# Forming the expert table of the last layer in wider pieces, and moving squares from VectorE to ScalarE

## The chip, the cores and the metric

The kernel runs on one core of one Trainium2 chip. The metric is the time of one execution on the device, in microseconds. An execution of the profiled kind also leaves a trace: its span runs from the first to the last instruction, and its own time is a little longer.

## The reference, cut to what matters

Three layers follow each other: a linear attention with complex decay, a soft mixture of experts, and a dense layer with a squared relu. The change touches only the last two products of the mixture and the dense layer:

```
c = softmax over 32 slots of (x @ phi)            # 3072 tokens x 32
x = c @ slot_out                                  # slot_out: 32 x 384
h = max(x @ w_in, 0)                              # w_in: 384 x 2048
out = (h * h) @ w_out                             # w_out: 2048 x 384
```

All arrays are fp32; the two weights arrive as 64-bit floats and are decoded to fp32 on the chip.

## The kernel before

The first stages (attention, and the experts that give `slot_out`) fill the first 297 us and are not touched. Their instructions are issued in an order written out by hand. The last layer is issued in program order, so that each engine has one queue in the order of the code below.

The last layer doesn't form x. Since x @ w_in = c @ (slot_out @ w_in), it forms G = slot_out @ w_in, 32 slots by 2048, once. To keep fp32 accuracy with products in a shorter format (F32R), each factor is split in a rounded part and a rest. G is stored in 128 partitions: 32 slots four times, rounded in partitions 0 to 63 and the rest in 64 to 127. cT, the transposed softmax of 512 tokens, has rounded, rest, rounded, rest in its four groups of 32 partitions. One product of G and cT over 128 partitions then gives all four cross terms.

- `make_G(f)` forms one block of 128 columns of G: three fp32 products (two instructions each) with soT, the transposed `slot_out` repeated four times by `slots`; then a ScalarE copy that rounds, and a VectorE subtraction that puts the rest in the upper half.
- `spread_c(g)` (VectorE) and `make_cT(g)` (four TensorE transposes, one ScalarE copy, two VectorE subtractions of 32 partitions) prepare the tokens of group g, 512 of 3072.
- The work is cut into 96 steps n: a group g of six and a block f of 16. `seq` runs over f = 0 to 7 for all six groups first (the first pass, n = 0 to 47) and then over f = 8 to 15 (the second pass).
- `up_last(n)` multiplies block f of G with cT of group g, takes relu to s and square to sh (rounded), both on ScalarE, and the square once more in full fp32, q, on VectorE, or on ScalarE for n = 1 to 7. `split(n)` makes sl = q - sh on VectorE.
- Step n then adds nine products to the three banks `po`: sh with the rounded and the rest of w_out (L784), sl with the rounded (L781). `up_last` runs two steps and `split` one step ahead of that.
- `weights_out` and the generator `beside_last` decode the weights of both products beside this (for each block of 128: ScalarE `size`, four VectorE steps, and for w_out also a ScalarE copy `woh` and a VectorE subtraction `wol`). In steps 0 to 3 one block of w_out is decoded per step; from step 4 the rest is taken in pieces, 2.4 per step. In that stretch G's blocks 8 to 15 are made too.
- After the eighth step of a group `po` is copied out (first pass) or added and stored (second pass).

The order of a step, cut:

```
if n: split(n + 1)
if n < HALF: make_G(f + 5), weights_out(f + 4)      # each while its argument is under 8
pieces of beside_last
if f == 3: spread_c(g + 1)
if f == 5: make_cT(g + 1, wide)
up_last(n + 2)
nine products into po
```

PSUM holds four banks for `ph` (G, cT and the products of `up_last`) and four for `po`; s and q have three buffers, sh and sl four.

Of the kernel before, what the change touches and what calls it, by code (L numbers as in the profile page):

```python
# [12 lines left out]
F32 = mybir.dt.float32  # L13
# [3 lines left out]
AF = mybir.ActivationFunctionType  # L17
ALU = mybir.AluOpType
# [12 lines left out]
NS = NE * SPE  # L31
# [79 lines left out]
HALF, PACE = 8, 2.4  # L111
# [169 lines left out]
def moe_kernel(ctx, tc, raw, cst, aT, qk, vv_d, phi, w1, w2, w_in, w_out, out):  # L281
    nc = tc.nc
    mm = nc.tensor.matmul
    tr = nc.tensor.transpose
    V = nc.vector

    const = ctx.enter_context(tc.tile_pool(name="const", bufs=1))
# [2 lines left out]
    cn = const.tile([128, NU, NS], F32, name="cn")  # L290
    flags = const.tile([128, 3, NTU], F32, name="flags")
    acc = const.tile([128, DM], F32, name="acc")
    soT = const.tile([128, 3, 4, NS], F32, name="soT")
    mrun = const.tile([128, 1], F32, name="mrun")
    srun = const.tile([128, 1], F32, name="srun")
    siT = const.tile([128, 3, NS], F32, name="siT")
# [6 lines left out]
    def act(*args, **kw):  # L303
        return nc.scalar.activation(*args, **kw)  # L304
# [200 lines left out]
    def pools(ph):  # L505
        def pool(name, bufs, **kw):
            return ph.enter_context(tc.tile_pool(name=name, bufs=bufs, **kw))
        return pool
# [26 lines left out]
    def finish(weights, psum, ps_b, hid, p_raw, p_d, used, swap, check):  # L535
# [8 lines left out]
        def bank():  # L544
            return ps_b.tile([128, 512], F32, name="pt")
# [39 lines left out]
        def slots(g):  # L585
            p = bank()
            for kc in range(3):
                tr(p[:, 128 * kc:128 * (kc + 1)], so[g][:, 128 * kc:128 * (kc + 1)], ident)
            for r in range(4):
                V.tensor_copy(  # L590
                    soT[:, :, r, 16 * g:16 * g + 16].rearrange("p k (j s) -> p k j s", j=4),
                    p[:, :DM].rearrange("p (k j s) -> p k j s", k=3, j=4)[:, :, :, :SPE])
# [15 lines left out]
        jobs = [(1, f) for f in range(HALF)] + [(o, f) for f in range(HALF, 16) for o in (0, 1)]  # L608
# [8 lines left out]
        def decode(n):  # L617

            o, f = jobs[n]
            if o:  # L620
                R["dw", n] = dst = R["dw"].tile([128, 1, DM], F32, name="dw")
            else:
                dst = wi[:, :, 128 * f:128 * (f + 1)]
            sl = slice(f, f + 1)
            return [fn for _, fn in f64_steps(p_d, lambda: R["raw", n], dst)] + [
                lambda: load_job(n + 3)] + [
                lambda: act(R["woh"][:, sl], R["dw", n], AF.Copy),
                lambda: V.tensor_tensor(out=R["wol"][:, sl], in0=R["dw", n], in1=R["woh"][:, sl], op=ALU.subtract)] * o

        def pieces(steps):  # L630
            for fn in steps:
                fn()
                yield

        def weights_out(n):
            steps = decode(n)
            for fn in steps[:4] + R.pop("parts", []) + steps[4:6]:
                fn()
            R["parts"] = steps[6:]

        def spread_c(g):
            R["c4", g] = R["c4"].tile([128, 4, 4, NS], F32, name="c4")
            V.tensor_copy(R["c4", g], cn[:, 4 * g:4 * g + 4].unsqueeze(2).to_broadcast([128, 4, 4, NS]))
# [44 lines left out]
        with phC, ExitStack() as ph:  # L688
            pool = pools(ph)
            G = pool("p_G", 1).tile([128, DFF], F32R, name="G")  # L690
            p_r = pool("p_r", 3)
            p_h = pool("p_h", 4)
            p_o = pool("p_o", 1)
            R["c"] = pool("p_cs", 1)
            ps_h = pool("ps_h", 4, space=PSUM)
            ps_o = pool("ps_o", 4, space=PSUM)
            sp, sq = {}, {}

            def wide():
                return ps_h.tile([128, 512], F32, name="ph")  # L700

            def make_G(f):
                if f >= 16:
                    return
                p = wide()[:, :128]
                for kc in range(3):
                    mm(p, soT[:, kc].rearrange("p r s -> p (r s)"), wi[:, kc, 128 * f:128 * (f + 1)], start=kc == 0, stop=kc == 2)
                dst = G[:, 128 * f:128 * (f + 1)]
                act(dst, p, AF.Copy)
                V.tensor_tensor(out=dst[64:], in0=p[64:], in1=dst[64:], op=ALU.subtract)  # L710

            seq = [(g, f) for fs in (range(HALF), range(HALF, 16)) for g in range(6) for f in fs]

            def beside_last():

                yield from pieces(R.pop("parts"))
                for m in range(HALF, len(jobs), 2):
                    yield from pieces(decode(m))
                    steps = decode(m + 1)
                    yield from pieces(steps[:3])  # L720
                    make_G(jobs[m][1])
                    yield from pieces(steps[3:])
            rest, paced = beside_last(), [0]

            def up_last(n):
                if n >= len(seq):
                    return
                g, f = seq[n]
                p = wide()
                mm(p, G[:, 128 * f:128 * (f + 1)], R["cT", g], start=True, stop=True)  # L730
                s = p_r.tile([128, 512], F32, name="s")
                act(s, p, AF.Relu)
                sh = p_h.tile([128, 512], F32R, name="sh")
                act(sh, s, AF.Square)
                q = p_r.tile([128, 512], F32, name="q")
                if not 0 < n < 8:
                    V.tensor_tensor(out=q, in0=s, in1=s, op=ALU.mult)  # L737
                else:
                    act(q, s, AF.Square)
                sq[n] = q, sh  # L740

            def split(n):
                if n >= len(seq):
                    return
                s, sh = sq.pop(n)
                sl = p_h.tile([128, 512], F32R, name="sl")
                V.tensor_tensor(out=sl, in0=s, in1=sh, op=ALU.subtract)  # L747
                sp[n] = sh, sl

            make_G(0)  # L750
            make_G(1)
            up_last(0)
            make_G(2)
            split(0)
            up_last(1)
            make_G(3)
            split(1)
            make_G(4)
            po, o = None, {}
            for n, (g, f) in enumerate(seq):  # L760
                if f % HALF == 0:
                    po = [ps_o.tile([128, 512], F32, name="po") for _ in range(3)]
                if n:
                    split(n + 1)
                if n < HALF:
                    if f + 5 < HALF:
                        make_G(f + 5)
                    if f + 4 < HALF:
                        weights_out(f + 4)
                while paced[0] < (n - 3) * PACE and next(rest, True) is None:  # L770
                    paced[0] += 1
                if f == 3 and n < 5 * HALF:
                    spread_c(g + 1)
                if f == 5 and n < 5 * HALF:
                    make_cT(g + 1, wide)
                up_last(n + 2)
                sh, sl = sp.pop(n)
                fst, lst = f % HALF == 0, f % HALF == HALF - 1

                def low(c):  # L780
                    mm(po[c], R["woh"][:, f, 128 * c:128 * (c + 1)], sl, start=False, stop=lst)  # L781
                for c in range(3):
                    for w in ("woh", "wol"):
                        mm(po[c], R[w][:, f, 128 * c:128 * (c + 1)], sh, start=fst and w == "woh", stop=False)  # L784
                    if lst:
                        low(c)
                if not lst:
                    for c in range(3):
                        low(c)
                if n == 20:  # L790
                    check()
                if lst:
                    for c in range(3):
                        if f < HALF:
                            o[g, c] = p_o.tile([128, 512], F32, name=f"o{g}{c}")
                            copy("D" if c == 1 else "A", o[g, c], po[c])
                        else:
                            V.tensor_tensor(out=o[g, c], in0=po[c], in1=o[g, c], op=ALU.add)
                            nc.sync.dma_start(out=out[128 * c:128 * (c + 1), 512 * g:512 * (g + 1)], in_=o[g, c])

    wi = ctx.enter_context(tc.tile_pool(name="p_wi", bufs=1)).tile([128, 3, DFF], F32, name="wi")
# [5 lines left out]
    with tc.manual_schedule():  # L807
# [395 lines left out]
        n = N_PRE  # L1203
# [42 lines left out]
        def check():  # L1246
            in_range.append(nc.values_load(count[:1, :1], min_val=0, max_val=128))
# [59 lines left out]
```

## Time and profile before

| what | value |
|---|---|
| three runs | 549.75, 550.99, 555.09 us; median 550.99 |
| profiled execution | 551.92 us, of which the span is 550.1 |
| mean granted TensorE clock | 0.991 of full speed |
| TensorE, VectorE, ScalarE busy | 520.2, 447.4, 361.9 us |
| last layer | about 297 us to 543 us |

Busy times are sums of the durations of an engine's instructions where they don't overlap; those of TensorE overlap their successors, so that the distance between starts, not the duration, is the price of one.

### The profile page before, as it was taken

The numbers are of one execution on the slowest core, as the hardware profiler recorded it, in microseconds if no ns is written. First come the engines' busy times: TensorE is split into PE (matmuls) and PEld (weight loads), VectorE is DVE, ScalarE is ACT, GpSimd is POOL, SyncE is SP. The second block draws the span as 40 slices with busy tenths as digits, with TensorE's granted clock in tenths as the row PEclk, the third lists the DMA queues.
The fourth block names the chain that finished last, engine by engine and source line by source line (L and its number), as shares of the span: only waits on it lengthen the run. The fifth ranks groups of instructions, "written<-read, shape, count | busy, mean of one in ns | idle before, by whom it ended". The sixth has DMA issues, their size and how long they took to land.

```text
span 550.1 us, 10120 instructions
## 1 busy us (share of the span) xinstructions
PE 520.2 (95%) x4006; PEld 417.1 (76%) x4006; DVE 447.4 (81%) x774; ACT 361.9 (66%) x664; POOL 0.2 (0%) x4
## 2 busy tenths in 40 slices
PE   0999999999999999999799979999999999999994
PEld 0998888888788787888336768777788888888883
DVE  4899999999999987885567978998998975777672
ACT  6799999999889876522034766757676655555550
POOL 0000000000000000000000000000000000000000
PEclk9999999999999999999899989999999999999998
DMA  6432533470462226739993312110210010111011
GB/s 213 144 117 90 184 93 130 128 292 23 121 236 90 74 87 206 299 139 422 421 397 130 87 57 59 57 58 31 58 57 30 0 58 0 60 57 57 2 57 63
DMA packets 23958, 67.15 MB, mean 122 GB/s; under 512 B 2144, under 2 KB 12256, under 8 KB 21856
## 3 DMA queue, kind: packets, MB, share of 16 engines
q1 hardware_dynamic: 23904, 66.44, 34.4%
q8 instruction: 33, 0.54, 0.4%
q14 instruction: 21, 0.17, 0.1%
HBM read 61.71 MB, written 4.72 MB: 121 GB/s over the span
## 4 chain that ended last, share of the span: by engine, by line
PE 86%; DVE 9%; ACT 1%; DMA 1%; issue 1%; SPq 1%; DVEq 0%; ACTq 0%
PE po L784 21%; PE po L781 10%; PE pt L1047 9%; PE pt L1095 8%; PE py L1110 6%; PE pS L1072 5%; PE pt L1228 5%; PE ph L730 4%; PE pt L939 3%; PE py L1115 3%; PE pt L557 2%; PE pt L1131 2%; DVE sl L747 2%; PE pt L572 1%; PE pt L334 1%; DMA a<-in_a_dram 1%
## 5 line engine op out<-in xcount | busy, mean ns | idle before, releaser
L784 PE MATMUL po<-sh,wol 128*128 128x512 f32 x288 | 114.4, 397 | 0.0
L784 PE MATMUL po<-sh,woh 128*128 128x512 f32 x288 | 114.2, 397 | 0.0
L304 ACT ACTIVATE s<-ph 128x512 f32<-128x512 f32 x96 | 57.2, 596 | 63.1 <-PE ph L730 62.9
L737 DVE TENSOR_TENSOR q<-s 128x512 f32<-128x512 f32 x89 | 61.3, 689 | 32.5 <-ACT s L304 32.1
L781 PE MATMUL po<-sl,woh 128*128 128x512 f32 x288 | 86.5, 395 | 0.0
L747 DVE TENSOR_TENSOR sl<-q,sh 128x512 fp32r<-128x512 f32 x96 | 66.3, 691 | 10.9 <-ACT q L304 1.3
L781 PEld LDWEIGHTS po<-sl,woh 128*128 128x128 f32 x288 | 54.4, 189 | 13.2 <-DVE sl L747 0.2
L784 PEld LDWEIGHTS po<-sh,wol 128*128 128x128 f32 x288 | 54.6, 189 | 12.9
L784 PEld LDWEIGHTS po<-sh,woh 128*128 128x128 f32 x288 | 54.6, 190 | 12.2 <-ACT o L304 0.3
L304 ACT ACTIVATE sh<-s 128x512 fp32r<-128x512 f32 x96 | 60.8, 633 | 3.1
L304 ACT ACTIVATE T<-pt 96x512 f32<-96x512 f32 x83 | 47.4, 593 | 11.0 <-PE pt L1047 10.5
L1095 PE MATMUL pt<-T,T 96*128 96x128 f32 x384 | 52.7, 280 | 0.0
L1095 PEld LDWEIGHTS pt<-T,T 96*128 96x128 f32 x384 | 46.6, 192 | 3.3 <-issue 2.6
L730 PE MATMUL ph<-cT,G 128*128 128x512 f32 x96 | 40.0, 417 | 4.5 <-DVE cT L653 4.4
L1110 PE MATMUL py<-am,v 128*48 128x128 f32 x384 | 40.9, 291 | 0.0
L1099 DVE TENSOR_TENSOR am<-pt,cs 128x512 f32<-128x512 f32 x48 | 32.8, 685 | 6.7 <-PE pt L1095 6.1
L939 PE MATMUL pt<-cs,t 128*128 128x128 f32 x144 | 23.6, 282 | 12.7 <-DVE t L893 12.7
L1115 PE MATMUL py<-T,S 96*48 96x128 f32 x320 | 31.3, 273 | 0.0
L1072 PEld LDWEIGHTS pS<-v,KN 128*96 128x96 f32 x320 | 29.4, 165 | 2.0 <-issue 2.0
L314 ACT ACT_TABLE_LOAD x23 | 29.5, 1283 | 1.1 <-PEq L1298 0.7
L1072 PE MATMUL pS<-v,KN 128*96 128x48 f32 x320 | 30.0, 247 | 0.0
L1047 PE MATMUL pt<-cs,KN 128*96 128x128 f32 x192 | 29.9, 278 | 0.0
(153 smaller groups left out, 856.7 us busy)
## 6 DMA issues: line engine op xcount, KB each, us to landing
w<-in_w_dram SPq DMA_DIRECT2D x16, 1536.0 KB, 11.5
qk<-in_qk_dram SPq DMA_DIRECT2D x24, 384.0 KB, 3.1
a<-in_a_dram SPq DMA_DIRECT2D x14, 576.0 KB, 4.6
raw<-in_wi_dram SPq DMA_DIRECT2D x16, 384.0 KB, 3.2
raw<-in_wo_dram SPq DMA_DIRECT2D x16, 384.0 KB, 3.1
v<-in_vn_dram SPq DMA_DIRECT2D x24, 192.0 KB, 2.6
out_dram<-o SPq DMA_DIRECT2D x18, 256.0 KB, 2.2
a<-in_a_dram SPq DMA_DIRECT2D x2, 384.0 KB, 5.0
```

What stands on the lines that cost most here:

```text
L304: return nc.scalar.activation(*args, **kw)
L730: mm(p, G[:, 128 * f:128 * (f + 1)], R["cT", g], start=True, stop=True)
L737: V.tensor_tensor(out=q, in0=s, in1=s, op=ALU.mult)
L747: V.tensor_tensor(out=sl, in0=s, in1=sh, op=ALU.subtract)
L781: mm(po[c], R["woh"][:, f, 128 * c:128 * (c + 1)], sl, start=False, stop=lst)
L784: mm(po[c], R[w][:, f, 128 * c:128 * (c + 1)], sh, start=fst and w == "woh", stop=False)
L939: tr(pe[:, C * j:C * (j + 1)], x[:, j, C * i:C * (i + 1)], ident)
L1047: tr(pt[:96, C * h:C * (h + 1)], X[:, 4 * g + h].rearrange("p c d -> p (c d)"), ident)
L1072: mm(pS[:96, D * h:D * (h + 1)], st["KN", u][:, h].rearrange("p c d -> p (c d)"), st["v", u][:, h], start=not seeded, stop=not seeded or h ...
L1095: mm(p[:, C * h:C * (h + 1)], st["T", u, 1, g][:, h], st["T", u, 0, g][:, h], start=True, stop=True)
L1110: mm(p[64 * w:64 * w + D, C * pr:C * (pr + 1)], st["v", u][:, h], st["am", u, h // 4][:, h % 4], start=True, stop=fst)
L1115: mm(p[64 * w:64 * w + D, C * pr:C * (pr + 1)], st["S", u][:, h], st["T", u, 0, h // 4][:, h % 4], start=False, stop=True)
```

## The change

G is formed for four blocks at once. soT now holds the slots twice, so the weights have 64 columns. Two blocks go to partitions 0 to 63 of one PSUM bank and the next two to partitions 64 to 127, 256 columns each, the products of the two halves alternating. For each half a ScalarE copy then writes the rounded part to partitions 0 to 63 of G and a VectorE subtraction the rest to 64 to 127. G(0) and G(4) are formed before step 0, the other two groups when the last of their four blocks of w_in is being decoded.

The square q goes to VectorE where n is a multiple of 3 or at least 45, otherwise to ScalarE. `spread_c` is moved from the fourth step of a group to the third (f = 2), `make_cT` from the sixth to the fifth (f = 4).

```diff
-    soT = const.tile([128, 3, 4, NS], F32, name="soT")
+    soT = const.tile([128, 3, 2, NS], F32, name="soT")
...
-            for r in range(4):
+            for r in range(2):
...
-            def make_G(f):
-                if f >= 16:
-                    return
-                p = wide()[:, :128]
+            def make_G(f, n=2):
+                p = wide()[:, :128 * n]
+                halves = [(p[64 * j:64 * j + 64], slice(128 * (f + n * j), 128 * (f + n * j + n))) for j in range(2)]
                 for kc in range(3):
-                    mm(p, soT[:, kc].rearrange("p r s -> p (r s)"), wi[:, kc, 128 * f:128 * (f + 1)], start=kc == 0, stop=kc == 2)
-                dst = G[:, 128 * f:128 * (f + 1)]
-                act(dst, p, AF.Copy)
-                V.tensor_tensor(out=dst[64:], in0=p[64:], in1=dst[64:], op=ALU.subtract)
+                    for q, sl in halves:
+                        mm(q, soT[:, kc].rearrange("p r s -> p (r s)"), wi[:, kc, sl], start=kc == 0, stop=kc == 2)
+                for q, sl in halves:
+                    act(G[:64, sl], q, AF.Copy)
+                    V.tensor_tensor(out=G[64:, sl], in0=q, in1=G[:64, sl], op=ALU.subtract)
...
-                    make_G(jobs[m][1])
+                    if jobs[m][1] % 4 == 3:
+                        make_G(jobs[m][1] - 3)
...
-                if not 0 < n < 8:
+                if n % 3 == 0 or n >= 45:
                     V.tensor_tensor(out=q, in0=s, in1=s, op=ALU.mult)
                 else:
                     act(q, s, AF.Square)
...
             make_G(0)
-            make_G(1)
             up_last(0)
-            make_G(2)
             split(0)
             up_last(1)
-            make_G(3)
+            make_G(4)
             split(1)
-            make_G(4)
...
-                if n < HALF:
-                    if f + 5 < HALF:
-                        make_G(f + 5)
-                    if f + 4 < HALF:
-                        weights_out(f + 4)
+                if n + 4 < HALF:
+                    weights_out(n + 4)
...
-                if f == 3 and n < 5 * HALF:
+                if f == 2 and n < 5 * HALF:
                     spread_c(g + 1)
-                if f == 5 and n < 5 * HALF:
+                if f == 4 and n < 5 * HALF:
                     make_cT(g + 1, wide)
```

## Rows read from the trace of the kernel before

**Rows 1.** Page: busy time, share of the span, instructions of each engine.

```profile
PE 520.2 (95%) x4006; PEld 417.1 (76%) x4006; DVE 447.4 (81%) x774; ACT 361.9 (66%) x664; POOL 0.2 (0%) x4
```

**Rows 2.** Chain that ended last, in order: start us, us, what, count.

```profile
132.72 0.44 PE pt L1047 x4
133.16 0.36 PE py L1110 x4
133.74 0.57 PE pt L1047 x4
...
134.66 0.22 PE py L1115 x4
...
284.94 0.86 PE pt L557 x16
...
328.55 0.67 PE ph L707 x6
329.22 0.23 PE ph L730
329.45 1.40 PE po L784 x6
330.85 0.70 PE po L781 x3
...
340.85 0.44 PE ph L648 x4
```

**Rows 3.** TensorE's products and transposes in order; in brackets its wait before.

```profile
297.06 1.58 PE L707 MATMUL ph<-wi,soT 128*128 128x128 f32 x12 [0.28 <-DVE soT L590]
298.71 0.50 PE L730 MATMUL ph<-cT,G 128*128 128x512 f32 x1
...
316.89 0.66 PE L648 MATMUL ph<-cs,c 128*128 128x128 f32 x4 [1.77 <-DVE c L643]
...
322.35 0.76 PE L730 MATMUL ph<-cT,G 128*128 128x512 f32 x1 [2.47 <-DVE cT L653]
...
326.05 0.40 PE L730 MATMUL ph<-cT,G 128*128 128x512 f32 x1
...
386.06 0.47 PE L730 MATMUL ph<-cT,G 128*128 128x512 f32 x1 [1.50 <-DVE cT L653]
...
443.01 0.40 PE L730 MATMUL ph<-cT,G 128*128 128x512 f32 x1
...
536.09 0.40 PE L730 MATMUL ph<-cT,G 128*128 128x512 f32 x1
```

**Rows 4.** Busy time of each engine in one stretch: PE, PEld, DVE, ACT, POOL, clock.

```profile
350.00:420.00 70.00, 68.01 (x312) 55.08 (x312) 64.20 (x116) 45.73 (x83) 0.00 (x0) 1.00 0.17 51
```

**Rows 5.** The same view after the longest gap; the seventh figure is the granted clock.

```profile
322.00:324.00 2.00, 1.65 (x4) 1.40 (x5) 1.94 (x5) 0.82 (x2) 0.00 (x0) 0.50 0.00 0
```

**Rows 6.** Groups by line from 160 us on: busy us, mean ns, idle before.

```profile
L737 DVE TENSOR_TENSOR q<-s 128x512 f32<-128x512 f32 x89 | 61.3, 689 | 32.5 <-ACT s L304 32.1
...
L710 DVE TENSOR_TENSOR G<-ph,G 64x128 fp32r<-64x128 f32 x16 | 4.6, 295 | 3.8 <-ACT G L304 3.4
...
L304 ACT ACTIVATE q<-s 128x512 f32<-128x512 f32 x7 | 4.3, 615 | 0.0
...
L304 ACT ACTIVATE G<-ph 128x128 fp32r<-128x128 f32 x16 | 4.1, 272 | 12.3 <-PE ph L707 12.3
```

**Rows 7.** VectorE in order of time, one lap: start us, us.

```profile
313.42 0.69 DVE L747 TENSOR_TENSOR sl<-q,sh 128x512 fp32r<-128x512 f32 x1
314.02 0.36 DVE L489 TENSOR_SCALAR dx<-raw 128x384 uint32<-128x384 uint32 x1
...
316.41 0.42 DVE L643 COPY c<-cn 128x512 f32<-128x512 f32 x1
316.75 0.69 DVE L747 TENSOR_TENSOR sl<-q,sh 128x512 fp32r<-128x512 f32 x1
```

**Rows 8.** ScalarE in order of time, before and at the copy of cT.

```profile
317.42 0.58 ACT L304 ACTIVATE s<-ph 128x512 f32<-128x512 f32 x1
318.04 0.63 ACT L304 ACTIVATE sh<-s 128x512 fp32r<-128x512 f32 x1
...
319.09 0.58 ACT L304 ACTIVATE cT<-ph 128x512 fp32r<-128x512 f32 x1
```

More of the change, by code (lines that the diff above doesn't have):

```diff
@@ L700, in wide @@
                 return ps_h.tile([128, 512], F32, name="ph")
-            def make_G(f):
-                if f >= 16:
-                    return
-                p = wide()[:, :128]
+            made = set()
+            def make_G(f, n=2):
+                p = wide()[:, :128 * n]
+                halves = [(p[64 * j:64 * j + 64], slice(128 * (f + n * j), 128 * (f + n * j + n))) for j in range(2)]
                 for kc in range(3):
-                    mm(p, soT[:, kc].rearrange("p r s -> p (r s)"), wi[:, kc, 128 * f:128 * (f + 1)], start=kc == 0, stop=kc == 2)
-                dst = G[:, 128 * f:128 * (f + 1)]
-                act(dst, p, AF.Copy)
-                V.tensor_tensor(out=dst[64:], in0=p[64:], in1=dst[64:], op=ALU.subtract)
+                    for q, sl in halves:
[3 more added lines that the diff above has]
+                    V.tensor_tensor(out=G[64:, sl], in0=q, in1=G[:64, sl], op=ALU.subtract)
+                made.update(range(f, f + 2 * n))
             seq = [(g, f) for fs in (range(HALF), range(HALF, 16)) for g in range(6) for f in fs]
@@ L728, in up_last @@
                 g, f = seq[n]
+                assert f in made
                 p = wide()
```

## The prediction

> **What bounds the kernel now.** I read the page's engine summary first, then busy time by windows of the last layer, then the chain that ended last, and then the separate instructions of TensorE, VectorE and ScalarE where that chain changes engine. The summary calls TensorE 95% busy [rows 1], which doesn't say where it waits: those durations overlap. The last layer tells more. A step of it (one `up_last` product and nine products into `po`) issues in 1.40 + 0.70 + 0.23 = 2.33 us in the chain [rows 2]; 40 steps in a row of the second pass take 536.09 - 443.01 = 93.08 us, 2.327 each [rows 3]. So the second pass is TensorE and nothing else, and nothing on another engine is worth anything there. The first pass is different. In 350 to 420 us VectorE is busy 64.20 of 70 us and ScalarE 45.73 [rows 4], and TensorE has real gaps: 1.77 us before the cT transposes, waiting for `spread_c`; 2.47 and 1.50 us before the product that needs the next cT [rows 3]. After the 2.47 us the granted clock is 0.50, the 1.2 GHz level [rows 5], and the step that begins there takes 326.05 - 322.35 = 3.70 us, 1.37 more than 2.33.
>
> I split the layer at the product of step 9 (326.05). Before it lies a stretch paced by VectorE, after it one paced by TensorE with a few gaps.
>
> **After step 9: the gaps.** From 326.05 to 536.09 are 210.04 us. TensorE's own work there: 86 steps x 2.327 = 200.12; eight `make_G` blocks at 0.67 = 5.36; four sets of transposes at 0.44 = 1.76 [rows 2]; 207.24 together. So the gaps, and the small delays around them, are worth 2.8 us, of which one row shows 1.50. Two edits reach them. Moving `make_cT` one step ahead gives cT 2.33 us more, against waits of 2.47 and 1.50. Moving squares: in the first 45 steps the new rule leaves 15 to VectorE, afterwards all; 66 on VectorE where there were 89, so 23 move, at 689 ns saved there and 615 ns added to ScalarE [rows 6]. In the 70 us window there are about 29 steps, 19 of them with the square moved: VectorE goes from 64.2 to 64.2 - 13.1 = 51.1, ScalarE from 45.7 to 57.4. Both then stand under TensorE's 70, so I count all 2.8 us as gained. Saving 16 us of VectorE is worth no more than that: it is cover, not path.
>
> **After step 9: G.** Eight blocks are made there, two groups of four. Now a block costs TensorE 0.67, four 2.67 [rows 2]: six instructions of 128 columns at 0.111 for each block. In the change four blocks are 12 instructions of 256 columns, with 64 columns of weights, alternating between the two halves of the output's partitions. Taken one after another they would need 12 x 0.222 = 2.67, nothing gained. Whether halves overlap, the earlier stages show. Four instructions of 128 columns into two 64-partition halves issue in 0.22 (L1115), half of 4 x 0.111, and sixteen of 256 columns into four 32-partition groups in 0.86 (L557), a quarter of 16 x 0.222 [rows 2]. So I take 12 x 0.111 = 1.33. Entering and leaving costs: the first such four after full-width work (L1110) take 0.36 where 0.22 is the pace, and the full-width four after them 0.57 where four elsewhere take 0.44 [rows 2]: 0.14 + 0.13 = 0.27. A group is then 1.6 us, 1.07 less than now; two groups 2.1. Bounds: 0.5 lost (no overlap, switches paid) to 2.7 gained (switches free).
>
> That row of 0.57 has its rule in the Trainium skill, "TensorEngine Tiling (Array Packing)", Key Properties: a change of tiling mode drains TensorE. It speaks against the change, and the trace agrees with it, at 0.27 for both ends.
>
> The evacuations: four ScalarE copies of 272 ns and four VectorE subtractions of 295 become two each of 64x256. By 689 at 512 columns and 295 at 128, a subtraction at 256 is about 426 ns (an estimate), a copy by 615 and 272 about 386 [rows 6]: slightly less work on both. The two of the second half read partitions 64 and up and write or combine with 0 and up, which no row shows; I take the same duration, bounds 0 to 0.3 us each, hidden behind `po` products after step 9. The second group is formed about one step before its first use (piece 109 of the paced work, 2.4 a step after step 3, gives step 49; `up_last` wants block 12 in step 50). Between lie the 2.09 us of `po`, against about 0.3 + 0.4 + 0.4 for its first half; hidden. In the queues ScalarE's copy waits for these products, with the relu of two steps ahead behind it, and VectorE's subtraction for the copy; both have more than that in hand. No DMA moves.
>
> **Before step 9.** Here VectorE sets the pace. Its lap in steps 0 to 3: subtraction `sl` 0.60 to the next start, five instructions of `weights_out` 316.41 - 314.02 = 2.39, once a copy `c` 0.34 [rows 7], and G's subtraction, 0.295 [rows 6], in the steps that will be without it. I lay the new order over these starts. The 0.28 wait for soT [rows 3] goes with two of four copies, so G begins at 296.8. From the first G to the first product are 298.71 - 297.06 = 1.65 us now [rows 3]: 0.67 for the block, 0.272 and 0.295 for copy and subtraction, so 0.41 of hand-overs. In the change they are 1.33 + 0.14 + 0.39 + 0.43 + 0.41 = 2.7, which puts the first product at 299.5, 0.8 later. The first `sl` ends about 302.1; the second waits for the copies and subtractions of `make_G(4)` and starts about 304.0. From there VectorE's laps run without G but with the square of step 3: `sl` starts about 307.0, 310.8, 314.1 (now 313.42 [rows 7]). `c` now stands before, not after, `weights_out(7)`: 314.2 instead of 316.8. The transposes therefore go at 314.3, though TensorE has by then waited about 0.6 for sh, 0.8 for `sl` and 2.0 for `c`. ScalarE's copy of cT stands behind woh, which waits for VectorE to finish block 7 (317.2): relu to square 0.62, square with q to the copy 1.05 [rows 8] put it at 318.2. VectorE's two cT subtractions follow at 318.8, 1.4 long (their end is bounded by the product at 322.35 that waited for them [rows 3]). The product of step 8 then goes at 320.2 instead of 322.35, after a gap of 0.9 us, and step 9's at 322.5 if the clock holds: 3.5 earlier, 1.37 of it the slow stretch. Bounds: 0 gained, if the 2.0 us gap lowers the clock as the 2.47 one did and the rest slips, to 4.5.
>
> **The sum.** 3.5 + 2.8 + 2.1 = 8.4 us. The profiled execution took 551.92 (span 550.1), so 543.5; the median of the three runs is 0.93 below that execution, so 542.6. About 1%, 5.5 us, is what a measurement of this kernel can tell from no change.
>
> **Rivals.**
> (a) The halves don't overlap. Each group costs 2.67 + 0.27: after step 9 that is 0.5 lost instead of 2.1 gained, and at the start the first product comes 1.3 later, with some of it behind VectorE: 1.6. The gain falls by 4.2 to 4.2 us: 546.8. Against it stand the 0.22 of L1115 and the 0.86 of L557 [rows 2]; for it, that 64 columns by 256 in two halves is a shape no row has. Chance 0.10. The Trainium skill has a rule this way ("TensorE: Matmul & The Clock Gate", Part 3): a weight load passes running products only where their row groups differ, and here they are the same; 0.22 for four instructions speaks against it.
> (b) The start gives nothing back: VectorE has two squares more (steps 3 and 6, 1.4 us), the first product is 0.8 late, and the 2.0 us gap takes the clock down. Then 2.8 + 2.1 = 4.9: 546.1. For it: the place is as crowded as before. Against: `c` comes 2.6 us sooner by its place alone. Chance 0.11.
> (c) ScalarE becomes the bound of the first pass, and the kernel is slower. Per step it has 57.4 / 29 = 2.0 us of work, TensorE 2.4. Decoding puts copies behind VectorE's last decode step on ScalarE's queue, and now relu, square and q of a step and so VectorE's next `sl` stand behind them. It decides from 0.4 us of such waits a step on; at 0.8 it loses 0.4 x 36 steps = 14.4 against 8.4 gained: 557.0 by the profile's 551.92 + 6.0 - 0.93. Against: from a product to the `sl` that needs it lie two whole steps, 4.65 us, and relu, square, q and `sl` take about 3.0. Chance 0.06.
>
> **How the numbers follow.** The forecast has 0.73. Nearly all of it lies over 1% faster, (a) and (b) lie within 1%, (c) beyond it on the other side: 0.72, 0.22 and 0.06. The range reaches from 540.3 (4.5 + 2.8 + 2.7 gained, and 0.3 of readings) to 549.0, which takes in (a) and (b) alone with some of both together (550.3), and leaves out (c).
>
> **What would show it.** G's twelve instructions at about 0.11 each, near 1.6 us with both switches; first product near 299.5; no gap over 1 us after step 9 and steps of 2.33 there; step 9's product about 322.5; VectorE near 51 and ScalarE near 57 of 70 us. A granted clock of 0.50 before step 9, G at 0.22 an instruction, or `sl` waiting for q on ScalarE step after step would make it wrong.

## The result and the profile after

The changed kernel takes 544.53 us in the median of six runs (544.21 to 545.52), the kernel before 550.43 in six; the ratio is 0.9881, with a 95% interval of 0.9851 to 0.9912. The forecast was 542.6, 540.3 to 549.0.

In the views PE is TensorE, PEld its weight loads, DVE VectorE and ACT ScalarE. A bracket gives how long the engine stood idle before the line, and what ended that.

The summary of the page of after:

```profile
PE 516.5 (95%) x3958; PEld 409.9 (75%) x3958; DVE 430.6 (79%) x739; ACT 371.1 (68%) x679; POOL 0.2 (0%) x4
```

VectorE has 16.8 us less than in [rows 1] and ScalarE 9.2 more, and the span went from 550.1 to 543.7. As before, the summary says that work moved and not what it bought.

TensorE's products in order, with its waits in brackets, in after; the first line of `ph<-cT` holds the products of steps 0 and 1:

```profile
297.88 1.51 PE L711 MATMUL ph<-wi,soT 128*64 128x256 f32 x12
300.38 0.74 PE L737 MATMUL ph<-cT,G 128*128 128x512 f32 x2 [0.98 <-DVE G L714]
301.05 1.51 PE L711 MATMUL ph<-wi,soT 128*64 128x256 f32 x12
302.50 0.50 PE L737 MATMUL ph<-cT,G 128*128 128x512 f32 x1
...
312.99 0.96 PE L782 MATMUL po<-sl,woh 128*128 128x512 f32 x3 [0.57 <-DVE sl L754]
315.73 0.74 PE L648 MATMUL ph<-cs,c 128*128 128x128 f32 x4 [1.77 <-DVE c L643]
316.14 0.75 PE L737 MATMUL ph<-cT,G 128*128 128x512 f32 x1
...
322.43 0.39 PE L737 MATMUL ph<-cT,G 128*128 128x512 f32 x1
...
324.75 0.40 PE L737 MATMUL ph<-cT,G 128*128 128x512 f32 x1
...
423.73 0.39 PE L737 MATMUL ph<-cT,G 128*128 128x512 f32 x1
...
426.14 1.52 PE L711 MATMUL ph<-wi,soT 128*64 128x256 f32 x12
427.59 0.50 PE L737 MATMUL ph<-cT,G 128*128 128x512 f32 x1
...
430.01 0.39 PE L737 MATMUL ph<-cT,G 128*128 128x512 f32 x1
...
530.08 0.40 PE L737 MATMUL ph<-cT,G 128*128 128x512 f32 x1
```

322.43 and 324.75 are the products of steps 8 and 9, 530.08 that of step 95. Set against [rows 3], the layer divides as the prediction divided it:

| stretch | before | after | change | forecast |
|---|---|---|---|---|
| first G to step 9's product | 326.05 - 297.06 = 28.99 | 324.75 - 297.88 = 26.87 | -2.12 | -3.2 (-3.5 with soT's 0.28) |
| step 9 to step 95 | 536.09 - 326.05 = 210.04 | 530.08 - 324.75 = 205.33 | -4.71 | -4.9 |
| together | 239.03 | 232.20 | -6.83 | -8.1 |

The spans differ by 6.4: the first G came 0.82 later in this execution, and the end after step 95 took 13.62 us instead of 14.01. The 0.82 arose in stages that the change doesn't touch; in the runs below, with the same code there, first G lies anywhere from 294.70 to 297.98. So I compare stretches of the last layer, which repeat far better than whole times.

Busy time of each engine in the window of [rows 4] and in the two that answer to [rows 5], in after (the seventh figure is the granted clock):

```profile
350.00:420.00 70.00, 70.00 (x314) 56.12 (x313) 54.66 (x99) 55.24 (x102) 0.00 (x0) 1.00 0.18 51
316.00:318.00 2.00, 2.00 (x9) 1.61 (x8) 1.93 (x5) 1.97 (x4) 0.00 (x0) 0.54 0.41 152
318.00:320.00 2.00, 2.00 (x7) 1.60 (x6) 1.81 (x4) 1.30 (x4) 0.00 (x0) 0.60 0.57 184
```

In this window TensorE no longer waits; VectorE has 54.66 of 70 us and ScalarE 55.24 (forecast 51 and 57). Before step 9 the clock still falls to its 1.2 GHz level, now behind the wait for c: the step that begins at 316.14 takes 3.97 us by its rows, where the slow step of before took 3.70.

ScalarE's two copies of the first G in after, and VectorE's two subtractions:

```profile
299.50 0.38 ACT L304 ACTIVATE G<-ph 64x256 fp32r<-64x256 f32 x1 [3.42 <-PE ph L711]
300.36 0.38 ACT L304 ACTIVATE G<-ph 64x256 fp32r<-64x256 f32 x1 [0.48 <-DVE G L714]
```

```profile
299.91 0.42 DVE L714 TENSOR_TENSOR G<-ph,G 64x256 fp32r<-64x256 f32 x1 [2.17 <-ACT G L304]
300.77 0.43 DVE L714 TENSOR_TENSOR G<-ph,G 64x256 fp32r<-64x256 f32 x1 [0.45 <-ACT G L304]
```

The durations are as estimated, and the half that reads partitions 64 and up costs the same as the other. But the four follow one another: the second copy waits for the first subtraction, though it reads the other half and writes other columns. No step of the prediction gives a time to that.

### The profile page after: what moved, and what is told of

It is laid out like the page before. It is cut to its first block, busy times and chain, and to the rows that moved or that the text cites. A ratio compares the mean times of both kernels' runs of the same rounds, so it can differ in the third digit from the quotient of the medians.

```text
span 543.7 us, 9991 instructions
## 1 busy us (share of the span) xinstructions
PE 516.5 (95%) x3958; PEld 409.9 (75%) x3958; DVE 430.6 (79%) x739; ACT 371.1 (68%) x679; POOL 0.2 (0%) x4
## 4 chain that ended last, share of the span: by engine, by line
PE 93%; DVE 3%; DMA 1%; ACT 1%; SPq 1%; issue 0%; DVEq 0%; ACTq 0%
PE po L785 24%; PE po L782 12%; PE pt L1048 9%; PE pt L1096 9%; PE py L1111 6%; PE pS L1073 5%; PE pt L1229 5%; PE ph L737 4%; PE pt L940 3%; PE py L1116 3%; PE pt L557 2%; PE pt L1132 2%; PE pt L572 2%; DMA a<-in_a_dram 1%; PE pt L334 1%; PE pt L371 1%
## 5 line engine op out<-in xcount | busy, mean ns | idle before, releaser
L754 DVE TENSOR_TENSOR sl<-q,sh 128x512 fp32r<-128x512 f32 x96 | 66.3, 691 | 19.7 <-ACT q L304 12.5
L744 DVE TENSOR_TENSOR q<-s 128x512 f32<-128x512 f32 x66 | 45.5, 690 | 28.8 <-ACT s L304 28.7
L1073 PEld LDWEIGHTS pS<-v,KN 128*96 128x96 f32 x320 | 29.4, 165 | 2.0 <-issue 2.0
```

What stands on the lines that cost most here:

```text
L1073: mm(pS[:96, D * h:D * (h + 1)], st["KN", u][:, h].rearrange("p c d -> p (c d)"), st["v", u][:, h], start=not seeded, stop=not seeded or h ...
```

## The experiments

The times of the first three columns are of one profiled execution each, by the same rows as above. "Clock" says whether the granted clock fell to 1.2 GHz before step 9. "Timed" is the median of the timed runs, and the ratio is to the kernel before, timed beside it: 550.43 us beside after, 552.19 beside x1 to x4, 550.86 beside x7 to x10, 551.58 beside the others. So ratios can be compared across the table, medians only among runs with the same kernel before beside them.

| run | first G to step 9 | step 9 to 95 | together | clock | timed | ratio, interval |
|---|---|---|---|---|---|---|
| before | 28.99 | 210.04 | 239.03 | fell | 550.43 | |
| after | 26.87 | 205.33 | 232.20 | fell | 544.53 | 0.9881, 0.9851 to 0.9912 |
| x14_same_again | 26.89 | 205.37 | 232.26 | fell | 544.42 | 0.9868, 0.9844 to 0.9892 |
| x1_squares_back | 25.43 | 210.25 | 235.68 | held | 547.70 | 0.9919, 0.9899 to 0.9939 |
| x2_cT_back | 29.88 | 207.14 | 237.02 | fell | 548.75 | 0.9938, 0.9909 to 0.9967 |
| x3_G_back | 26.67 | 207.11 | 233.78 | fell | 546.28 | 0.9898, 0.9880 to 0.9916 |
| x4_halves_in_turn | 27.26 | 206.39 | 233.65 | fell | 544.89 | 0.9862, 0.9838 to 0.9887 |
| x9_full_width | 25.82 | 207.89 | 233.71 | held | 545.48 | 0.9907, 0.9881 to 0.9934 |
| x7_G4_later | 27.44 | 205.94 | 233.38 | held | 545.53 | 0.9907, 0.9870 to 0.9943 |
| x8_c_sooner | 26.24 | 205.94 | 232.18 | held | 545.01 | 0.9878, 0.9828 to 0.9927 |
| x10_start | 26.67 | 205.60 | 232.27 | held | 544.49 | 0.9874, 0.9824 to 0.9923 |
| x13_kept_warm | 26.23 | 205.94 | 232.17 | held | 544.16 | 0.9867, 0.9839 to 0.9895 |
| x6_two_banks | 26.43 | 205.33 | 231.76 | fell | 544.04 | 0.9863, 0.9843 to 0.9883 |
| x12_joined | 24.99 | 205.60 | 230.59 | held | 543.77 | 0.9856, 0.9836 to 0.9876 |

x14 is the changed kernel unaltered:

> The changed kernel as it is, once more, as the measure of what one profile is worth beside the others of this call. Theory: TensorE's order is fixed, so from step 9 to step 95 it is again 205.3 within 0.6 us, and first G to step 9's product 26 to 27, depending on whether the wait of 1.77 us for c lowers the granted clock (26.9 with 0.5 granted behind it, about 26.0 without). Rival (the start's numbers differ by more from one execution to the next, so that differences of 1 us between the other runs say nothing): outside 25.5 to 27.3.

It came out 0.02 and 0.04 us from the first profile, with the clock falling at the same place. x8 and x13, both with the clock held, also agree to 0.01 us. So differences of some tenths mean something, where the timed medians, which carry the earlier stages, move by a microsecond. But whether the clock fell moves step 9's product by 0.6 us (26.87 in after, 26.23 in x13, whose order is the same and whose clock held), and the stretch behind it by as much the other way. The first two columns are therefore compared only among runs with the same clock; "together" holds for all.

### Each part undone

```diff
-                if n % 3 == 0 or n >= 45:
+                if not 0 < n < 8:
```

> The changed kernel with the old rule for the squares: ScalarE has them in steps 1 to 7, VectorE elsewhere. Theory: without the moved squares VectorE needs about 2.55 us a step in the first pass where TensorE needs 2.43, so from step 9 to step 95 (205.3 us in the changed kernel, 210.0 before) waits of 1 to 4 us for sl come back, while the start gains, because VectorE loses two squares before step 8: first G to step 9's product 25 to 26.5 (26.9 in the changed kernel). In all 544 to 548 us. Rival (the place of cT alone took the gaps away, the squares only buy idle time on VectorE): 205.3 again from step 9 on and 543 to 544 us in all.

In this execution the clock didn't fall. Against x13, where it held too, step 9's product came 0.8 sooner, inside the range expected, and the stretch behind it took 4.3 more (4.9 more than in after), a little over the 1 to 4 expected; together 3.5 more. The window of [rows 4] in this run, and the waits of 326 to 425 us (total, times, longest):

```profile
350.00:420.00 70.00, 68.66 (x304) 53.99 (x303) 63.51 (x112) 44.83 (x81) 0.00 (x0) 1.00 0.18 51
```

```profile
ACT woh L304 <- DVE dw L502: 12.1, 7, 3.0
ACT dy L304 <- DVE wi L502: 10.1, 6, 3.2
...
PE po L785 <- ACT o L304: 1.7, 2, 1.3
...
PE po L782 <- DVE sl L754: 0.8, 1, 0.8
```

VectorE is as full as before, at 63.51. It holds up TensorE less by `sl` itself than by way of ScalarE, which stands idle in its queue behind decode steps that wait for VectorE, and then copies `o` out of PSUM late: 22 us of such idle time here, 7.6 in the same window of after. The moved squares are cover that the first pass needs; the rival falls.

```diff
-                if f == 2 and n < 5 * HALF:
+                if f == 3 and n < 5 * HALF:
                     spread_c(g + 1)
-                if f == 4 and n < 5 * HALF:
+                if f == 5 and n < 5 * HALF:
                     make_cT(g + 1, wide)
```

> The changed kernel with spread_c and make_cT in the old steps (fourth and sixth of a group). Theory: with VectorE at 55 of 70 us no cT comes late after step 9 even so, 205 to 206 us there; the start loses, because c and cT come later for step 8: first G to step 9's product 28 to 29.5 (26.9). In all 545.5 to 547.5 us. Rival (the gaps after step 9 went by the place of cT): waits for cT of 1 us or more return at two or more groups, 207.5 us or more from step 9 on.

The start lost 3.0, and step 9 to 95 lost 1.8: between the theory's 205 to 206 and the rival's 207.5. VectorE's window, and TensorE's waits for cT behind step 9:

```profile
350.00:420.00 70.00, 68.71 (x305) 54.40 (x305) 53.36 (x95) 54.38 (x100) 0.00 (x0) 1.00 0.17 51
```

```profile
384.30 0.47 PE L737 MATMUL ph<-cT,G 128*128 128x512 f32 x1 [0.98 <-DVE cT L653]
...
403.91 0.47 PE L737 MATMUL ph<-cT,G 128*128 128x512 f32 x1 [0.32 <-DVE cT L653]
```

So a VectorE that is busy 53 of 70 us doesn't by itself bring cT in time: in two of the four groups one step, 2.33 us, was too short for transposes, copy and two subtractions in two queues. Place and cover are both needed, and my theory that cover alone would do is wrong here. At 4.8 us together this edit is worth most. It moves `spread_c` and `make_cT` at once; what each does alone wasn't run.

For x3 the old `make_G`, its places, and soT four times were put back:

```diff
-            def make_G(f, n=2):
+            def make_G(f):
...
-            make_G(0)
-            up_last(0)
-            split(0)
-            up_last(1)
-            make_G(4)
-            split(1)
+            make_G(0); make_G(1); up_last(0); make_G(2); split(0)
+            up_last(1); make_G(3); split(1); make_G(4)
```

> The changed kernel with G formed block by block as before (soT four times), squares and cT as changed. Theory: eight blocks after step 9 cost TensorE 0.67 each where two groups cost 1.63 each, so 207.4 us from step 9 on (205.3); at the start the first product is sooner and VectorE's second sl too, but seven more TensorE and VectorE pieces stand in steps 0 to 2: first G to step 9's product 26 to 28 (26.9). In all 546 to 547.5 us. Rival (the halves gain nothing, the time came from VectorE): 205.3 from step 9 on and 544.5 in all.

As expected: 1.8 lost after step 9 and nothing at the start. G's new form is worth 1.6. Undone one at a time the three parts cost 3.5, 4.8 and 1.6, in sum 9.9 against 6.8 gained together. A sum above the whole means that part of the gain needs two edits at once, and is lost with either: squares and place of cT. With G's 1.6 taken off what x2 and x1 still gain on before (2.0 and 3.4), squares alone would be worth about 0.4 and the place of cT alone about 1.8, against 5.2 for both in x3 (an estimate; neither was run alone on the kernel before).

### Why the wide G is cheaper

```diff
-                for kc in range(3):
-                    for q, sl in halves:
+                for q, sl in halves:
+                    for kc in range(3):
                         mm(q, soT[:, kc]..., wi[:, kc, sl], start=kc == 0, stop=kc == 2)
```

> The changed kernel with the products of G ordered by half: three of the lower half, then three of the upper, the same twelve instructions. Theory: the halves' products overlap only where they alternate; in turn they take 0.222 each, so a group costs 2.7 to 3.0 us where it costs 1.63: 207.5 to 208.2 us from step 9 to step 95 (205.3), and 1 to 2.5 us more at the start. In all 547.5 to 550 us. Rival (twelve wide instructions with 64 columns of weights are cheap by themselves, or TensorE is not the bound there): 205.3 from step 9 on, 544.5 in all.

It lost 1.06 after step 9, where 2.2 to 2.9 were expected. A group of this run:

```profile
425.32 2.00 PE L711 MATMUL ph<-wi,soT 128*64 128x256 f32 x12
427.25 0.50 PE L737 MATMUL ph<-cT,G 128*128 128x512 f32 x1
```

Twelve instructions in 1.93 us are 0.16 each: neither 0.222 nor the 0.12 of after (1.45 for twelve), so my theory that halves overlap only where they alternate is wrong. That left two explanations, and x9 tells them apart: two blocks at once over the full width, with soT four times.

```diff
+                dst = G[:, 128 * f:128 * (f + n)]
                 for kc in range(3):
-                    for q, sl in halves:
-                        mm(q, ..., wi[:, kc, sl], ...)
+                    mm(p, ..., wi[:, kc, 128 * f:128 * (f + n)], ...)
```

> The changed kernel with G formed for two blocks at once over the full width: soT four times, six instructions with 128 columns of weights and 256 columns streamed, no halves. The run with the halves in turn gave 0.16 an instruction, not 0.22, so a second theory stands: an instruction's price is the larger of loading its weight columns and streaming its columns, and 128 by 128 was priced by its weights. Theory A (streaming 256 columns hides behind loading 128): a pair of blocks costs TensorE 0.67 to 0.75, the changed kernel's 205.3 us from step 9 to step 95 stays within 0.5. Theory B, the prediction's (only overlapping halves bring the price down, 256 columns at full width cost 0.22): a pair costs 1.33 and it is 207 to 207.5 us.

207.89: theory B. One of the four pairs behind step 9 in this run:

```profile
426.64 1.46 PE L710 MATMUL ph<-wi,soT 128*128 128x256 f32 x6
427.74 0.58 PE L735 MATMUL ph<-cT,G 128*128 128x512 f32 x1
...
430.25 0.40 PE L735 MATMUL ph<-cT,G 128*128 128x512 f32 x1
```

427.74 - 426.64 = 1.10 to the next product, and that step takes 0.18 more than 2.33: 1.28 for six, 0.21 an instruction. Four pairs for two groups are 1.86 us more; against x13, whose clock held as here, the stretch took 1.95 more. That 207.89 lies 0.4 us over theory B's range comes from a wait of 0.62 for ScalarE's copy of `o`, right behind step 9, which belongs to the next part. So width buys nothing by itself, and the price of 256 columns falls to 1.45 / 12 = 0.12 because the two halves run beside each other. The starts of the single records say the same: in x9 they lie 0.216 us apart, in after each half has one every 0.216 us, and the two halves start within 0.01 us of each other. In x4 an instruction out of that pace, which I take for the second half's first, starts 0.49 us after the first half's first, beside its third, and from there both halves go on at 0.216: that delay is the 0.48 us between 1.45 and 1.93. So the halves overlap in turn too, only later.

### The start

Four edits of the first steps, none of which changes the code of step 9 and later:

```diff
 x7:         make_G(4)      # moved: behind weights_out(4) in step 0
 x8:         if n == 2: spread_c(1)      # moved: ahead of weights_out(6)
 x13:        for _ in range(7 * (g == 1)): mm(p[:, :C], ident, ident, start=True, stop=True)   # in make_cT
 x10:        x7 and x8, and q of steps 3 and 6 on ScalarE
```

> The changed kernel with make_G(4) behind weights_out(4) in step 0 instead of ahead of split(1). Theory: VectorE's second sl no longer waits for q and two copies and subtractions that follow each other (1.11 and 0.45 us idle ahead of it), so its laps begin 0.6 us sooner or more: first G to step 9's product 26.0 to 26.5 (26.9), from step 9 on 205.3. Rival (the start is paced by TensorE or by ScalarE's copies): 26.9 again. In all 544 to 545 us.

27.44, and 1.2 worse than x13, whose clock held as here; together 1.2 worse than after. ScalarE and TensorE in this run:

```profile
304.58 0.38 ACT L304 ACTIVATE G<-ph 64x256 fp32r<-64x256 f32 x1 [2.48 <-DVE G L714]
```

```profile
306.30 0.50 PE L786 MATMUL po<-sh,woh 128*128 128x512 f32 x1 [1.19 <-ACT sh L304]
```

Behind `weights_out`, the first subtraction of G comes late on VectorE; ScalarE's second copy waits 2.48 for it, with the relu and square of step 2 behind it, and TensorE waits 1.19 for sh. My theory looked at VectorE alone and fell.

> The changed kernel with the first spread_c ahead of weights_out(6) in step 2, not behind it. Theory: TensorE's wait of 1.77 us for c goes to 0.6 or less, the granted clock holds its upper level, and the wait moves on to cT's subtractions or to sl: first G to step 9's product 25.5 to 26.3 (26.9). Rival (the clock falls whatever fills that stretch, or VectorE's later work comes as late as before): 26.9 or more. From step 9 on 205.3 either way.

> The changed kernel with seven products of the identity with itself (1.55 us of TensorE) ahead of the first make_cT's transposes, into the same bank, so that they fall into the wait for c. Theory: the granted clock holds 1.0 and the product of step 8 then waits for cT's subtractions instead: first G to step 9's product 25.8 to 26.2 (26.9 where the clock fell), from step 9 on 205.3 to 206. Rival (the clock's fall cost nothing, the chain through cT sets that time): 26.9 with the clock at 1.0 throughout.

Up to step 9 both theories held; for the layer as a whole the rivals did. In x8 the wait for c is gone, in x13 it is filled, and both keep the granted clock at 1.00 through the start; step 9's product came 0.6 sooner, at 26.24 and 26.23. But the total is 232.18 and 232.17, against 232.20 in after and 232.26 in x14. TensorE in x13:

```profile
314.45 0.66 PE L650 MATMUL ph<-cs,c 128*128 128x128 f32 x4 [0.20 <-DVE c L643]
...
320.44 0.47 PE L739 MATMUL ph<-cT,G 128*128 128x512 f32 x1 [0.67 <-DVE cT L655]
...
326.61 0.50 PE L787 MATMUL po<-sh,woh 128*128 128x512 f32 x1 [0.58 <-ACT o L304]
```

The time given back at c is taken again at cT's subtractions and, two steps on, at ScalarE's copy of `o`, which frees the `po` bank. VectorE's subtractions of cT and ScalarE's copies of `o`, in after and then in x13:

```profile
320.19 1.39 DVE L653 TENSOR_TENSOR cT<-ph,cT 32x512 fp32r<-32x512 f32 x2 [0.38 <-ACT cT L304]
327.27 1.07 ACT L304 ACTIVATE o<-po 128x512 f32<-128x512 f32 x2
```

```profile
318.90 1.39 DVE L655 TENSOR_TENSOR cT<-ph,cT 32x512 fp32r<-32x512 f32 x2 [0.36 <-ACT cT L304]
325.98 1.07 ACT L304 ACTIVATE o<-po 128x512 f32<-128x512 f32 x2
```

From first G (297.88 and 296.61) these are 22.3 and 29.4 us in both. So the fall of the clock, which lengthened one step by 1.64 us, cost the kernel nothing: VectorE and ScalarE kept their times, and TensorE ran at 1.2 GHz while it would otherwise have waited for them.

> The changed kernel with three edits of the start together: make_G(4) behind weights_out(4), the first spread_c ahead of weights_out(6), and the squares of steps 3 and 6 on ScalarE too. Theory: VectorE's chain to step 8 is 2 us shorter and no gap lowers the clock: first G to step 9's product 23.5 to 25, from step 9 on 205.3, in all 541.5 to 543.5 us. Rival (ScalarE, which now has every square there, or TensorE's own 22.6 us become the pace at once): 25.5 or more and 544 in all.

26.67 and 232.27, as the rival said. The edit of x7 is in it, and with it TensorE's 1.19 for sh; the other two edits gain 1.1 on x7, which is what x7 had lost.

```diff
-                p = wide()[:, :128 * n]
-                halves = [(p[64 * j:64 * j + 64], ...
+                p = [wide()[:, :128 * n] for _ in range(2)]
+                halves = [(p[j][64 * j:64 * j + 64], ...
```

> The changed kernel with the two halves of make_G in two PSUM banks instead of one. Theory: ScalarE's second copy waits for VectorE's first subtraction (0.48 us each time) because both read one bank's tile; in two banks it follows the first copy at once, VectorE's second sl starts 0.4 to 0.9 us sooner after G(4): first G to step 9's product 0.3 to 0.9 less than the same kernel's. From step 9 on 205.3 to 206. Rival (the wait comes from G's tile, not from the bank): the second copy still waits 0.48 and the start is as before.

ScalarE and VectorE at the first G of this run:

```profile
298.30 0.79 ACT L304 ACTIVATE G<-ph 64x256 fp32r<-64x256 f32 x2 [3.40 <-PE ph L711]
```

```profile
298.71 0.88 DVE L714 TENSOR_TENSOR G<-ph,G 64x256 fp32r<-64x256 f32 x2 [2.15 <-ACT G L304]
```

The two copies follow each other at once and so do the subtractions: the wait came from the shared PSUM tile and not from G's. Each tile has a bank of its own here, so which of the two asks for the wait isn't shown. The start is 0.44 sooner, with the clock falling as in after.

> The changed kernel with the squares of steps 3 and 6 on ScalarE, the first spread_c ahead of weights_out(6), and the halves of make_G in two banks; make_G(4) stays where it is. Theory: VectorE's chain to step 8 is 1.4 us shorter by the squares and c and cT no longer come late: first G to step 9's product 24 to 25.3, from step 9 on 205.3 to 206, so 1 to 2.5 us less than the changed kernel in the same call. Rival (whatever is taken from VectorE at the start, cT behind four decoded blocks sets step 8): 26 and no difference that the times show.

24.99 and 230.59, 1.6 us under after and under x14, with the clock at 1.00 throughout the start. One wait of over a microsecond is left before step 9, the old one for cT:

```profile
317.29 0.47 PE L737 MATMUL ph<-cT,G 128*128 128x512 f32 x1 [1.44 <-DVE cT L653]
```

By the layer's rows, of one execution, this version beats both kernels. By the timed runs (543.77 against 544.42 for x14 timed beside it, with intervals that overlap widely) it can't be told from after; against before its ratio is 0.9856.

The traces say where its 1.6 us come from. Starts in us from first G; the forecast's are counted from its 296.8:

| start of | forecast | after | x13 | x8 | x6 | x12 |
|---|---|---|---|---|---|---|
| VectorE's second `sl` | 7.2 | 7.57 | 7.56 | 7.56 | 7.12 | 7.11 |
| VectorE's first subtraction of cT | 22.0 | 22.30 | 22.29 | 22.29 | 21.87 | 21.05 |
| TensorE's product of step 9 | 25.7 | 26.87 | 26.23 | 26.24 | 26.43 | 24.99 |
| ScalarE's first copy of `o` | none | 29.39 | 29.37 | 29.38 | 28.96 | 27.79 |
| TensorE's product of step 11 | 30.35 | 31.76 | 31.75 | 31.75 | 31.32 | 30.16 |

The last forecast is 25.7 and two steps of 2.327. In each of these runs the product of step 11 follows the first copy of `o` by 2.4 us. Two banks save 0.45 up to the second `sl`. From there to cT's subtractions it is 14.7 us, and 13.9 in x12, without the square of step 3; from those to `o` 7.1, and 6.7 without the square of step 6. That is 0.45, 0.8 and 0.35, x12's 1.6. x1, where ScalarE has these two squares as well, shows the same 13.9 and 6.7. In x8 `c` comes 2.4 us sooner than in after and cT's subtractions don't move: the place of the first `c` isn't on that path.

## Why the prediction was right, and where not

The direction and the range held; the gain came out smaller, 6.8 of 8.4 us in the last layer of the profiled executions and 5.9 in the medians. The order of the terms didn't hold: the start was forecast as the largest (3.5, then 2.8 and 2.1) and came out no larger than G (2.1, with 2.6 for the gaps and 2.1 for G). By its own sum the lower end of the range would have been 550.99 - 10.0 - 0.3 = 540.7 and not 540.3; nothing hangs on that.

**What bounds it.** Right for what lies behind step 9. The steps of the second pass didn't move (2.33 in both), and the gain lies where the gaps and G lay.

**The gaps after step 9, 2.8 us.** Right in size: 86 x 2.327 + 2 x 1.63 + 4 x 0.44 = 205.14 of work leaves 0.2 of gaps in 205.33. The prediction credited both edits without dividing; x1 and x2 show that neither alone suffices. That the stretch met the forecast so closely is in part luck: where the clock held before step 9 (x7, x8, x13), the wait for `o` made it 205.94.

**G after step 9, 2.1 us.** Right: a group takes 1.53 in its step (427.59 - 423.73 = 3.86 from product to product) and 0.09 in the next (430.01 - 427.59 = 2.42), 1.63 where 1.6 was forecast, and x3 loses 1.8 without it. Rival (a), no overlap, is refuted by x9, at 0.21 for what halves do in 0.12. The rule that the prediction put beside it, from the Trainium skill ("TensorE: Matmul & The Clock Gate", Part 3), that weight loads pass running products only where row groups differ, would have made the alternating halves slow; the trace, with 0.12 an instruction, speaks against it.

**Before step 9, 3.5 us.** This is the term that was mis-sized: it measured 2.1, or 2.3 with 0.22 that soT's copies saved ahead of G. "The product of step 8 then goes at 320.2 ... and step 9's at 322.5 if the clock holds" failed in two places.

The first is VectorE's chain. The prediction gave no time to the second copy's wait for the first subtraction, so the second `sl` starts 7.6 us after first G and not 304.0 - 296.8 = 7.2; the laps behind it then came as laid out, to cT's subtractions at 22.3, not 22.0. Two banks (x6) give 0.44 back.

The second is the clock, and behind it the copy of `o`. The granted clock fell, which the prediction had named as a sign that it is wrong, and which the lower bound allowed for; it puts step 9's product 0.6 later. But x13 and x8 show that holding the clock gains nothing in the end: by the product of step 11 all three stand at 31.75 or 31.76, 1.4 later than the 30.35 that the forecast comes to. In x13, with the clock held, 0.53 of that is there at step 9 and the rest, 0.86 over 2.33, falls in step 10, where TensorE waits for the bank that ScalarE's copy of `o` has to free. The prediction has no such wait; it let VectorE pace the stretch only up to step 9, and VectorE and ScalarE pace it to step 10.

Rival (b) had the two squares at 1.4 us; off VectorE they give 0.8 and 0.35 (x12). The forecast had the first in its laps; the second stands ahead of `o`. The argument against (b), that `c` comes sooner by its place, carries less than it seemed: sooner still, in x8, it moves neither cT nor step 11.

**Rival (c).** ScalarE rose to 55.24 of 70 us and from 326 to 425 us VectorE waited for its q 12 times, 12.5 us in all, yet TensorE's products show no wait there. It was the reverse in x1: with the squares on VectorE, ScalarE waits for VectorE's decode steps 22 us in 100, and TensorE for ScalarE.

## What to carry to other kernels

Two edits that each look like "more slack" can be worth little alone and much together, if one gives an operand more time and the other takes load off the queue that makes it; test them separately and together. A stall that is filled is gained only if the next late one lies far behind it: follow the stretch to a point behind the next late ones, not to the stall. Here the point was step 11 and not step 9, where the prediction and I had cut the layer. If two engines empty one PSUM tile in parts, look whether the parts wait for each other; two tiles may cost nothing but a bank.

## What the runs showed of the hardware

- Instructions of 256 fp32 columns into two 64-partition halves of one bank cost 0.12 us each where they alternate, 0.16 where six of one half precede six of the other, and 0.21 over the full width. Within one half, and over the full width, their starts lie 0.216 us apart; two halves keep that pace side by side, even when issued in turn, which I had not expected.
- A copy from PSUM partitions 64 and up to SBUF partitions 0 and up took the same 0.38 us as one without a shift, and the subtraction 0.42 to 0.43 either way.
- TensorE's wait for c was followed by a granted clock at the 1.2 GHz level in after, x14 and x4 (1.77 us), x6 (1.78) and x3 (1.91), and not in x2 and x7 (1.76), x1 and x9 (1.78); x2's fell later, behind a wait of 2.10 for cT. In x7 waits of 1.19 and 0.85 us stood ahead of it in steps 0 to 4, in x3 the view shows none there. So neither its length nor the gaps before it told which.
- One step at the lower level took 3.97 us where others take 2.33, and it cost the layer nothing, because VectorE and ScalarE set the time of what came next (232.20 us with it, 232.17 and 232.18 without).
